# Two copies per x tile, a fourth PSUM pair for longer, and a new split of the wk copies

## The chip, the cores and the metric

The kernel runs on one core of one Trainium2 chip. The time is the device time of one execution in microseconds (us), and lower is better. A profile's span is about 1.8 us shorter than the time of its execution (288.8 us and 290.67 us for the kernel before). The effect looked for here is a few tenths of a per cent, so most of this study reads stretches of single traces, where a stall of 0.2 us is visible. The total time of one execution scatters by more than that.

## The reference

The kernel computes a gated mix of a linear attention (branch A) and an FFN (branch B) over the same input `x` of 2048 tokens by 640.

```python
# cut: helpers and the set-up of inputs (all bfloat16)
q, k, v = split(x @ wqkv)                       # 32 heads of 20
pq, pk  = q @ w_phi[h], k @ w_phi[h]
phi_q   = concat(softmax(pq), softmax(-pq))     # phi_k likewise
kv, z   = sum_s phi_k (x) v, sum_s phi_k
o       = (phi_q @ kv) / (phi_q . z + 1e-6)
a       = o @ wo
b       = (silu(x @ w_gate) * (x @ w_up)) @ w_down
g       = sigmoid((x * gate_w).sum(-1))
out     = g * a + (1 - g) * b
```

## The kernel before

Everything is issued from one list of loads and one list of operations. A tracker adds semaphore waits by what each operation reads and writes, PSUM by whole banks. The skill's rule is of the same kind: the Trainium skill, "PSUM — Partial Sum Buffer", section "PSUM bank collisions raise a hardware error", wants accesses of two engines kept apart by bank and quadrant, not by address. The rule explains why the change puts the two copies of an x tile in two banks.

The letters that matter: `H` warm matmuls on constants, `X t` transposes x tile t on TensorE, `U t.c` is part c of the v projection of tile t (two matmuls, one chunk of 128 input columns), `V` a whole v tile, `M m` premultiplies block m of wk with w_phi, `F b.k` is an FFN tile, `K` a k tile, `E` a step of the kv sum, `I` takes the fourth PSUM pair out of the ring because the kv sum needs it.

```python
LOADS = """
x0 w0 x1 w1 x2 w2 x3 w3 w4 f0 h k0 k1 t4 k2 k3 k4 t5 t6 t7 ... t15 q0 q1 q2 q3
q4 f1 f2
"""
# f0, f1, f2: columns 0 to 255, 256 to 895, 896 to 1727 of w_gate and w_up
ORDER = """
H0 H1 H2 H3 H4 H5 H6 H7 H8 H12 G X0 H9 H10 H11 U0.0 X1 H13 U0.1 U1.0 U1.1 X2 U0.2 U1.2 U2.0 U2.1
X3 U2.2 U0.3 U1.3 U2.3 U0.4 U1.4 U2.4 V3 Y F0.1 M1 i3 M0 I F0.0 M2 V4 M3 M4 K0 K1 S0 V6 V5 S1 P0
# ... cut
R2 E5 K9 S8 P7 R1 E6 K10 S9 V12 P8 E7 P9 K11 S10 P10 F0.8 R3 F1.10 E8 E9 K12 E10 S11 S12 K14 S14
# ... cut
"""
# ... cut
    def xpose(t):
        pr = next_pair()                  # least recently used pair of PSUM banks
        o = bankbf(2 * pr, 640)
        transposes([(o[:, c * P:(c + 1) * P], xs[:, t, c * P:(c + 1) * P]) for c in range(5)])
        copy("dve", xT[:, t, :, :].rearrange("p c k -> p (c k)"), o)
# ... cut
    def warm():
        pr = next_pair()
        c = nc.const_aps.tensor(1.0, [P, P], BF16)
        def fn():
            for _ in range(NWARM):        # NWARM = 2
                last = pe.matmul(bank(2 * pr, 0, P), lhsT=c, rhs=c, start=True, stop=True)
            return last
        run("pe", fn, [], [bank(2 * pr, 0, P)])
# ... cut
    def premult(which, m):
        # ... six small matmuls into both banks of a pair
        copy("dve" if which and m % 2 == 0 else "act", wqk[:, which, m, :]..., halves(pr))
# ... cut
    def kv_begin():
        ring["n"] = 3
```

The softmax here doesn't subtract the row's maximum and nothing guards it: scores larger than these inputs give would overflow.

## Time and profile before

| | kernel before |
|---|---|
| time | 290.92 us (median of 3; 290.85 to 291.63) |
| span of the profile | 288.81 us |
| TensorE (PE) busy | 285.2 us, 99% |
| PE's waits, as listed | 1.6 us, 0.8 of it at the start |

The profile's page, part 1 (busy us, share of the span, instructions) and part 4 (the chain that ended last):

```profile
PE 285.2 (99%) x1977; PEld 174.7 (60%) x1977; DVE 162.8 (56%) x241; ACT 147.5 (51%) x251; POOL 160.5 (56%) x125
...
PE 96%; DMA 2%; DVE 1%; SPq 0%; ACT 0%; issue 0%
```

TensorE is the bound. A matmul's busy time is modelled, so 99% doesn't mean that TensorE is at its peak, but a change can gain only where TensorE stands still or runs at half rate. The list of PE's waits (what waited, for what, us in total, times, longest):

```profile
PE ps L471 <- PEq L773: 0.8, 1, 0.8
PE ps L294 <- DMA wvg<-in_A_wqkv_dram: 0.4, 2, 0.2
PE ps L294 <- DVE wqk L318: 0.2, 1, 0.2
PE ps L294 <- DVE xT L318: 0.2, 1, 0.2
```

Where they lie shows in the timeline of PE (start, busy us, what, count, idle time before it):

```profile
4.76 0.61 PE L294 MATMUL ps<-wvg,xT 128*128 128x320 bf16 x2 [0.23 <-DMA wvg<-in_A_wqkv_dram]
5.21 0.44 PE L306 MATMUL ps<-ident,xs 128*128 128x128 bf16 x5
5.49 0.28 PE L471 MATMUL ps<-const-bfloat16-1.0 128*128 128x128 bf16 x2
5.60 0.44 PE L294 MATMUL ps<-wvg,xT 128*128 128x320 bf16 x2
6.24 0.72 PE L294 MATMUL ps<-wvg,xT 128*128 128x320 bf16 x4 [0.20 <-DVE xT L318]
6.80 0.44 PE L306 MATMUL ps<-ident,xs 128*128 128x128 bf16 x5
7.40 1.27 PE L294 MATMUL ps<-wvg,xT 128*128 128x320 bf16 x8 [0.17 <-DMA wvg<-in_A_wqkv_dram]
...
12.09 1.24 PE L294 MATMUL ps<-xT,wg 128*128 128x512 bf16 x5
...
19.43 0.47 PE L294 MATMUL ps<-wbd,wT 128*128 128x140 bf16 x6 [0.23 <-DVE wqk L318]
```

The bracketed idle time counts only from the modelled end of the matmul before. From start to start, beyond what a matmul takes when nothing stalls (138 ns for 320 columns), the stall before 6.24 is 0.36 us, that before 7.40 is 0.33 us and that before 19.43 is 0.39 us. The line at 12.09 is the first FFN tile, F0.1. I shall use it, the first k tile (19.75) and the tile F0.8 (52.15) as marks.

### The profile page before, as it was taken

What the parts mean: (1) busy time and instruction counts of PE and PEld (TensorE: products, weight loads), DVE (VectorE), ACT (ScalarE), POOL (GpSimd) and SP (SyncE); (2) the same over time, 40 slices, a digit from 0 to 9 for tenths busy, and PEclk for the clock granted to TensorE, in tenths of its full rate; (3) what the DMA queues carried; (4) which work ended last, traced back from release to release, by engine and by line L of the source; (5) the groups of instructions that cost most, each with busy time, mean ns of one, the idle gap of its engine ahead of it and who ended that gap; (6) DMA issues with size and microseconds to landing.
All of it is one profiled execution on the core that took longest, in us unless ns stands there. A gap on an engine that the chain in (4) does not pass through costs nothing.

```text
span 288.8 us, 4885 instructions
## 1 busy us (share of the span) xinstructions
PE 285.2 (99%) x1977; PEld 174.7 (60%) x1977; DVE 162.8 (56%) x241; ACT 147.5 (51%) x251; POOL 160.5 (56%) x125
## 2 busy tenths in 40 slices
PE   8999999999999999999999999999999999999997
PEld 6667777675644445557775546675454446656776
DVE  1256757486468987769992385980316799200000
ACT  1368768676674556574354663224675452234112
POOL 8276899879544798844733348450663649601000
DMA  6966789000010497302373102061020004410101
GB/s 214 174 119 129 108 229 353 5 2 1 0 49 0 75 330 137 70 10 41 62 141 85 20 0 51 2 134 57 2 50 0 2 1 82 92 45 0 48 23 48
DMA packets 48942, 21.61 MB, mean 75 GB/s; under 512 B 39384, under 2 KB 48792, under 8 KB 48920
## 3 DMA queue, kind: packets, MB, share of 16 engines
q1 hardware_dynamic: 48190, 20.62, 31.3%
q10 hardware_dynamic: 730, 0.68, 0.7%
q8 instruction: 16, 0.26, 0.4%
q14 instruction: 6, 0.05, 0.1%
HBM read 9.29 MB, written 2.62 MB: 41 GB/s over the span
## 4 chain that ended last, share of the span: by engine, by line
PE 96%; DMA 2%; DVE 1%; SPq 0%; ACT 0%; issue 0%
PE ps L294 96%; DMA wvg<-in_A_wqkv_dram 2%; SPq L348 0%; DVE wqk L318 0%; DVE hT L326 0%; ACT hT L312 0%; PE ps L306 0%; DVE osb L718 0%
## 5 line engine op out<-in xcount | busy, mean ns | idle before, releaser
L322 POOL TENSOR_TENSOR hT<-hT,us 128x512 bf16<-128x512 bf16 (+1 forms) x56 | 65.6, 1182 | 66.8 <-DVE hT L326 66.6
L326 DVE SCALAR_TENSOR_TENSOR hT<-hT,ps 128x512 bf16<-128x512 bf16 (+1 forms) x56 | 37.5, 683 | 73.5 <-ACT hT L312 61.2
L294 PE MATMUL ps<-xT,wg 128*128 128x512 bf16 x260 | 64.6, 379 | 0.0
L294 PE MATMUL ps<-xT,wu 128*128 128x512 bf16 x260 | 64.6, 379 | 0.0
L294 PE MATMUL ps<-wd,hT 128*128 128x320 bf16 (+2 forms) x462 | 63.9, 295 | 0.0
L312 ACT ACTIVATE hT<-ps 128x512 bf16<-128x512 f32 (+2 forms) x60 | 35.8, 596 | 46.5 <-PE ps L294 46.4
L322 POOL TENSOR_TENSOR ph<-eq,qc 128x1320 bf16<-128x1320 bf16 x16 | 42.4, 2648 | 26.1 <-DVE qc L631 24.0
L294 PEld LDWEIGHTS ps<-wd,hT 128*128 128x128 bf16 x462 | 44.5, 98 | 17.5 <-issue 0.2
L294 PE MATMUL ps<-wqk,xT 128*128 128x320 bf16 x320 | 47.7, 299 | 0.1
L294 PEld LDWEIGHTS ps<-xT,wu 128*128 128x128 bf16 x260 | 25.4, 98 | 30.7
L294 PEld LDWEIGHTS ps<-xT,wg 128*128 128x128 bf16 x260 | 25.0, 98 | 27.8 <-ACT oT L312 0.8
L312 ACT ACTIVATE osb<-ps,omg 128x640 bf16<-128x640 f32 (+2 forms) x17 | 12.9, 758 | 53.7 <-PE ps L294 53.7
L322 POOL TENSOR_TENSOR ekr<-ekr,krec 128x1280 bf16<-128x1280 bf16 x16 | 37.4, 2358 | 5.1 <-DVE krec L336 5.1
L294 PEld LDWEIGHTS ps<-wqk,xT 128*128 128x128 bf16 x320 | 30.5, 98 | 13.3 <-ACT us L312 0.5
L312 ACT ACTIVATE us<-ps 128x512 bf16<-128x512 f32 (+1 forms) x56 | 33.2, 593 | 0.3 <-POOL hT L322 0.2
L312 ACT ACTIVATE eq<-ps 128x640 bf16<-128x640 f32 x32 | 22.4, 704 | 17.3 <-POOL ph L322 10.4
L333 DVE TENSOR_REDUCE ksum<-ekr 128x64 f32<-128x1280 bf16 x16 | 23.5, 1470 | 10.4 <-ACT ekr L312 10.4
L312 ACT ACTIVATE ekr<-ps 128x640 bf16<-128x640 f32 x32 | 22.3, 704 | 8.6 <-PE ps L294 8.1
L294 PE MATMUL ps<-wvg,xT 128*128 128x320 bf16 (+1 forms) x160 | 24.6, 301 | 0.6 <-DMA wvg<-in_A_wqkv_dram 0.4
L333 DVE TENSOR_REDUCE qz<-eq 128x64 f32<-128x1280 bf16 x16 | 23.7, 1478 | 2.2 <-ACT eq L312 2.2
L294 PE MATMUL ps<-wog,oT 128*128 128x320 bf16 (+2 forms) x165 | 24.7, 294 | 0.0
L333 DVE TENSOR_REDUCE qw<-ez 128x64 f32<-128x1280 bf16 x16 | 23.6, 1477 | 0.0
(73 smaller groups left out, 188.6 us busy)
## 6 DMA issues: line engine op xcount, KB each, us to landing
out_dram<-osb SPq DMA_DIRECT2D x15, 160.0 KB, 1.9
wd<-in_B_w_down_dram SPq DMA_DIRECT2D x1, 2080.0 KB, 10.4
wg<-in_B_w_gate_dram SPq DMA_DIRECT2D x1, 1040.0 KB, 9.5
wu<-in_B_w_up_dram SPq DMA_DIRECT2D x1, 1040.0 KB, 10.5
wg<-in_B_w_gate_dram SPq DMA_DIRECT2D x1, 800.0 KB, 5.6
wu<-in_B_w_up_dram SPq DMA_DIRECT2D x1, 800.0 KB, 7.2
wog<-in_A_wo_dram SPq DMA_DIRECT2D x2, 375.0 KB, 7.1
wvg<-in_A_wqkv_dram SPq DMA_DIRECT2D x4, 160.0 KB, 4.5
```

The lines of the kernel that those rows point to most:

```text
L294: last = pe.matmul(o, lhsT=l, rhs=r, start=st, stop=sp_, skip_group_check=sk)
L312: return run("act", lambda: act.activation(o, i, func, scale=scale), rd, [o])
L322: return run(e, lambda: eo.tensor_tensor(o, a, b, op), [a, b], [o])
L326: return run("dve", lambda: dve.scalar_tensor_tensor(out=o, in0=a, scalar=s, in1=b, op0=op0, op1=op1), rd, [o])
L333: return run("dve", lambda: dve.tensor_reduce(o, i, AX.X, ALU.add), [i], [o])
```

## The change

The intent is to remove the stalls above. Each of x0, x1, x2 leaves PSUM in two copies, of one chunk and of four chunks, so that the first v part of the tile can follow after the small copy; the v parts are reordered for it, and one pair of warm matmuls goes. The fourth PSUM pair stays in the ring until just before the first kv sum. Of the five wk copies VectorE (DVE) takes blocks 0 and 3 instead of 0, 2 and 4, and ScalarE (ACT) the others.

```diff
 ORDER = """
-H0 H1 H2 H3 H4 H5 H6 H7 H8 H12 G X0 H9 H10 H11 U0.0 X1 H13 U0.1 U1.0 U1.1 X2 U0.2 U1.2 U2.0 U2.1
-X3 U2.2 U0.3 U1.3 U2.3 U0.4 U1.4 U2.4 V3 Y F0.1 M1 i3 M0 I F0.0 M2 V4 M3 M4 K0 K1 S0 V6 V5 S1 P0
+H0 H1 H2 H3 H4 H5 H6 H7 H8 H12 G X0 H9 H10 U0.0 X1 H11 U1.0 U0.1 U1.1 X2 U2.0 U0.2 U1.2 U2.1
+X3 U2.2 U0.3 U1.3 U2.3 U0.4 U1.4 U2.4 V3 Y F0.1 M1 i3 M0 F0.0 M2 V4 M3 M4 K0 K1 I S0 V6 V5 S1 P0
 # ... cut
-    ring = {"n": 4, "lru": [0, 1, 2, 3]}
+    ring = {"n": 4, "lru": [0, 1, 3, 2]}
 # ... cut
     def xpose(t):
         pr = next_pair()
-        o = bankbf(2 * pr, 640)
-        transposes([(o[:, c * P:(c + 1) * P], xs[:, t, c * P:(c + 1) * P]) for c in range(5)])
-        copy("dve", xT[:, t, :, :].rearrange("p c k -> p (c k)"), o)
+        for c0, c1 in (((0, 1), (1, 5)) if t < 3 else ((0, 5),)):
+            o = bankbf(2 * pr + (c0 > 0), 640)
+            transposes([(o[:, c * P:(c + 1) * P], xs[:, t, c * P:(c + 1) * P]) for c in range(c0, c1)])
+            copy("dve", xT[:, t, c0:c1, :].rearrange("p c k -> p (c k)"), o[:, c0 * P:c1 * P])
 # ... cut
-        copy("dve" if which and m % 2 == 0 else "act", wqk[:, which, m, :].rearrange("p (b c) -> p b c", b=2), halves(pr))
+        copy("dve" if which and m in (0, 3) else "act", wqk[:, which, m, :].rearrange("p (b c) -> p b c", b=2), halves(pr))
```

## The prediction

> **What bounds the kernel now.** TensorE: the page gives PE 285.2 of 288.8 us busy (99%), and the chain that ended last is 96% PE. The list of PE's waits holds 1.6 us: 0.8 at the start, 0.4 for wvg loads, 0.2 for an xT copy, 0.2 for a wqk copy. Behind 19.43 us the chain is practically PE alone, so only what lies before can shorten the kernel.
>
> From the PE timeline before 20 us (start to start; an unstalled v part, two matmuls, takes 0.276 us):
> - Last warm matmul 4.22, first v part 4.76: the load of w0 lands at 4.63; the x0 copy had ended at 4.42.
> - v part 5.74, next 6.24: 0.36 us stall for the x1 copy (0.49 us on DVE).
> - Last x2 transpose 7.02, next v part 7.40: 0.33 us stall for w2, which lands at 7.36.
> - The last wk block (19.43) waits 0.39 us for the DVE copy of wk block 2 (18.47 to 19.28), since only three PSUM pairs are in the ring.
>
> **What the change does.**
> 1. Split copies. For x0 this frees nothing, w0 gates it. x1's first copy (estimate from the 128x5 copy, 0.18 us, and the 128x640 one, 0.49: 0.24 us) lets U1.0 start near 5.76; x2's lets U2.0 run about 7.14 to 7.41. The gate at 7.36 stays, but U2.0 (0.276 us) has moved in front of it. The removed warm pair (0.11 us) also lies in front and is worth nothing. DVE gains about 0.18 us per tile while idle over 1 us. Worth: 0.26 us.
> 2. Fourth pair until the first kv sum. By the ring's order the last wk block then takes the pair of the FFN tile before it, whose DVE reader ended at 18.55 (18.27 shifted), and can start near 18.77; its own load landed at 18.54, so it just holds. Worth: nearly all of 0.39 us. From the third k tile on the ring is the same up to renaming of pairs.
> 3. New split of copies (DVE 0, 3; ScalarE 1, 2, 4). DVE's block 3 ends near 19.8, ScalarE's block 4 near 20.0; k tile 0 needs them at about 19.9 and 20.2. Narrow; worth 0 by itself.
>
> Everything after moves with PE; the later xT and wTq loads keep at least 0.4 us of slack. Sum: 0.65 us, 0.2%.
>
> **Prediction: 290.3 us, range 289.6 to 290.9.** Faster by over 2%: 1%; within 2%: 98%; slower by over 2%: 1%.
>
> **What would show it.** No PE wait for wqk; the wait for w2 at about 7.36 remains, with U2.0 just before it; PE 0.26 us earlier at the first FFN tile (11.8 instead of 12.09), 0.65 us earlier at the first k tile (19.1 instead of 19.75). Span about 288.15.
>
> **What would make it wrong.** The Trainium skill, "TensorE: Matmul & The Clock Gate", Part 1, says that TensorE starts at half clock and is released after a busy window of about 3.4 us that runs freely. The trace agrees: warm matmuls 107 ns apart, transposes 56 ns apart from 5.2 us. The new order has one warm pair fewer before w0 lands (0.2 us more idle); were the release delayed by a window, over 1 us would be lost. A small copy dearer than 0.24 us, or a k tile waiting for block 3 or 4, would eat 0.1 to 0.3. The three times of before spread over 0.78 us, more than the gain, so the sign may not show.

## The result, and the profile after

The changed kernel takes 290.69 us (median of 6; 290.24 to 291.01), the kernel before 290.86 us (median of 6; 290.07 to 291.63). The ratio is 0.9996, with a 95% interval from 0.9976 to 1.0015: the same. All ratios here are the mean time of one kernel's fast runs over that of the other's of the same rounds, so they are not quite the ratio of the medians quoted. Executions over 1.5% slower than the fastest of the same kernel are left out of the means.

The page of the changed kernel, parts 1 and 4:

```profile
PE 284.7 (99%) x1975; PEld 174.2 (60%) x1975; DVE 162.6 (56%) x243; ACT 148.1 (51%) x252; POOL 160.5 (56%) x125
...
PE 93%; SPq 4%; DMA 2%; issue 0%; DVE 0%
```

PE's waits in the changed kernel:

```profile
PE ps L472 <- PEq L774: 0.8, 1, 0.8
PE ps L294 <- issue: 0.6, 1, 0.6
PE ps L294 <- DMA wvg<-in_A_wqkv_dram: 0.6, 1, 0.6
```

The waits for the xT and wqk copies are gone from the list. One wait for the weights w0 is left, and there is a new one of 0.6 us that the list puts down to "issue", which means that the profile shows no releaser. The chain now leads back through the issues of SyncE's queue (SPq 4%) and a DMA instead of through PE alone. Next, PE's timeline of the changed kernel, the lines that answer to those of before:

```profile
4.67 0.43 PE L294 MATMUL ps<-wvg,xT 128*128 128x320 bf16 x2 [0.57 <-DMA wvg<-in_A_wqkv_dram]
4.94 0.44 PE L306 MATMUL ps<-ident,xs 128*128 128x128 bf16 x5
5.22 0.28 PE L472 MATMUL ps<-const-bfloat16-1.0 128*128 128x128 bf16 x2
5.48 1.00 PE L294 MATMUL ps<-wvg,xT 128*128 128x320 bf16 x6
6.32 0.44 PE L306 MATMUL ps<-ident,xs 128*128 128x128 bf16 x5
6.85 1.27 PE L294 MATMUL ps<-wvg,xT 128*128 128x320 bf16 x8
...
11.56 1.24 PE L294 MATMUL ps<-xT,wg 128*128 128x512 bf16 x5
...
15.43 1.24 PE L294 MATMUL ps<-xT,wu 128*128 128x512 bf16 x5
16.75 0.49 PE L294 MATMUL ps<-wbd,wT 128*128 128x140 bf16 x6
...
18.45 0.79 PE L294 MATMUL ps<-wbd,wT 128*128 128x140 bf16 x12
19.08 2.88 PE L294 MATMUL ps<-wqk,xT 128*128 128x320 bf16 x20
```

F0.1 starts 0.53 us earlier (11.56 for 12.09). Half of this is not the split's: x1's transposes already start 0.27 us earlier (4.94 for 5.21), because w0 landed 0.09 us earlier and the first v part ran at full rate in this execution (0.27 us to the transposes instead of 0.45 us). From x1's transposes to F0.1 it is 6.62 us instead of 6.88 us, so 0.26 us are gained there, as predicted. The stalls for the xT copies are shorter there, not gone: read from start to start, U1.0 still stalls 0.15 us (5.48) and U2.0 0.26 us (6.85), each behind its small copy; the list doesn't show them for the reason given above. The prediction had counted on such a rest. The last two wk blocks now run as one piece (18.45, x12). The first k tile starts 0.67 us earlier (19.08 for 19.75). So the change did what it was meant to do. Between 15.43 and 16.75 there is a stall of 0.24 us that wasn't there before: the load of wk block 2 landed at 16.70 in this execution, and at 15.90 in the trace of before.

The gain then disappears at one place. PE around F0.8, the first tile to read the third set of FFN columns, in the kernel before:

```profile
50.79 1.52 PE L294 MATMUL ps<-wqk,xT 128*128 128x320 bf16 x10
52.15 1.24 PE L294 MATMUL ps<-xT,wg 128*128 128x512 bf16 x5
```

and in the changed kernel:

```profile
50.12 1.52 PE L294 MATMUL ps<-wqk,xT 128*128 128x320 bf16 x10
52.22 1.24 PE L294 MATMUL ps<-xT,wg 128*128 128x512 bf16 x5 [0.58 <-issue]
```

The k tile before it starts 0.67 us earlier, F0.8 itself 0.07 us later. In the trace's semaphore events PE's sequencer waits from 50.07 to 52.17 us for the load of the last columns of w_up, which lands at 52.13. In the kernel before the same wait ended at 51.47 (landing 51.44), while PE still had work queued until 52.15. So the slack was about 0.65 us there, and the shift used it up; in addition the load came 0.69 us later. It took both: with the load as early as in the trace of before, F0.8 would have lost about 0.05 us (an estimate: TensorE could have begun it at 52.15 - 0.67 = 51.48 us, and 0.09 us, the time from landing to first matmul in after, behind a landing at 51.44 is 51.53 us). In the 12 traces of the table below the last large load lands between 51.10 and 52.50 us. The Trainium skill, "DMA: Bandwidth & Descriptors", section "Why a DMA increments its semaphore by 16 and not by 1", says that a transfer runs on up to 16 engines that finish independently, and that only the full count means that all has landed. The trace agrees: of the 16 increments of this load 14 came by 50.34, one at 50.98 and the last at 52.13. The three large loads before it in this trace show the same lag of 1.8 us between the 14th increment and the last (44.31, 46.56 and 49.44 us are their landings), so what was late was late from the first of them on.

One thing was overlooked, and no run tests it. F0.8 begins with five w_gate matmuls, whose columns had landed at 49.44 us, but `fitem` passes the w_gate and the w_up matmuls to one call of `mm`, which waits for both loads before the first of them. The w_gate matmuls take 1.08 us. Had the wait for w_up stood behind them, it would have been over before they were (an estimate: they could have run from 51.48 to 52.56 us, and the load landed at 52.13).

Behind F0.8 the two traces are alike: 234.56 us to the start of the last matmul in each, and 2.1 us from there to the end. The sum of differences is -0.53 (to F0.1) -0.14 (to the first k tile) +0.74 (to F0.8) = +0.07 us, which is the difference of the spans, 288.88 against 288.81.

### The profile page after: what moved, and what is told of

It is laid out like the page before. It is cut to its first block, busy times and chain, and to the rows that moved or that the text cites. A ratio compares the mean times of both kernels' runs of the same rounds, so it can differ in the third digit from the quotient of the medians.

```text
span 288.9 us, 4883 instructions
## 1 busy us (share of the span) xinstructions
PE 284.7 (99%) x1975; PEld 174.2 (60%) x1975; DVE 162.6 (56%) x243; ACT 148.1 (51%) x252; POOL 160.5 (56%) x125
## 4 chain that ended last, share of the span: by engine, by line
PE 93%; SPq 4%; DMA 2%; issue 0%; DVE 0%
PE ps L294 93%; SPq L347 2%; DMA wT<-in_A_wqkv_dram 2%; SPq L348 1%; DVE osb L719 0%; PE ps L306 0%
```

## The experiments

Theory L (load gate): the shift is real, and TensorE gives it back by waiting for the last FFN load. Theory C (clock): in every trace of the table below TensorE runs at half rate at first and at full rate later; I call the step the release of the clock. The changed order has lost the idle time in which a late release of TensorE's clock did no harm, so part of the gain is lost in some executions. The rival of both is that the early shift is a chance of one execution, or that the gain is lost elsewhere.

All kernels gave correct results. Each has five rounds (five or six executions with the profiled one), and the first execution of each was the profiled one. The first four ran on one chip, the next four on another and the last four on a third, each batch with its own 11 runs of the kernel before. This table splits the traces; it is read from start to start. The profiled executions of a_after_again and e_warm_more were slow ones and are left out. "Full rate from" is the first of two matmuls in a row that follow each other at full rate (56 ns for 128 columns, against 107 at half rate; the first two matmuls of all, about 60 ns apart in every trace, don't count). "x1 to F0.1" is the part of F0.1's time from the first x1 transpose on.

| kernel | x order | full rate from | w0 lands | F0.1 | x1 to F0.1 | to first k tile | to F0.8 or its stand-in | to last matmul | tail | span |
|---|---|---|---|---|---|---|---|---|---|---|
| before | old | 5.21 | 4.63 | 12.09 | 6.88 | 7.66 | 32.40 | 234.56 | 2.10 | 288.81 |
| c_before_loads | old | 5.19 | 4.63 | 12.14 | 6.95 | 7.66 | 32.40 | 234.56 | 2.09 | 288.86 |
| h_pair_only | old | 6.31 | 3.94 | 12.04 | 7.05 | 7.27 | 32.39 | 234.57 | 2.09 | 288.37 |
| after | new | 3.69 | 4.54 | 11.56 | 6.62 | 7.52 | 33.14 | 234.56 | 2.09 | 288.88 |
| b_after_loads | new | 4.59 | 3.92 | 11.18 | 6.59 | 7.27 | 32.39 | 234.56 | 2.33 | 287.75 |
| d_after_tiles | new | 4.76 | 4.31 | 11.36 | 6.61 | 7.50 | 32.39 | 234.56 | 2.09 | 287.92 |
| g_split_only | new | 4.96 | 4.04 | 11.35 | 6.69 | 7.66 | 32.41 | 234.56 | 2.09 | 288.07 |
| i_after_warm | new | 5.70 | 3.97 | 11.91 | 6.84 | 8.05 | 32.40 | 234.56 | 2.09 | 289.02 |
| b2_after_loads | new | 6.38 | 4.22 | 12.02 | 7.18 | 7.27 | 32.39 | 234.56 | 2.23 | 288.48 |
| j_best | new | 7.10 | 4.41 | 12.46 | 7.38 | 7.39 | 32.40 | 234.56 | 2.10 | 288.91 |
| k_cold | new | 8.80 | 4.29 | 12.93 | 8.02 | 7.27 | 32.39 | 234.56 | 2.10 | 289.25 |
| f_warm_less | new | 4.65 | 4.03 | 12.54 | 7.89 | 7.27 | 32.39 | 234.56 | 3.74 | 290.51 |

### First batch: is it the load?

**a_after_again.** No edit.

> The changed kernel again, for the same chip as the other three. Load theory: TensorE is about 0.6 to 0.7 us ahead of the kernel before up to 51 us, then waits for the last of the four large FFN loads (w_up, columns 896 to 1727), which lands at 51.4 to 52.2 us whatever TensorE does; the first FFN tile that reads it starts within 0.1 us of the landing; span 288.4 to 289.0. Rival (the gain was never there, the early shift is a chance of this one execution): first k tile not about 0.6 us earlier than 19.75. Ratio 0.9985 to 1.000 under either.

Measured: the profiled execution took 608.59 us. In it even two neighbouring FFN groups of five matmuls start 2.33 us apart, against 1.08 us in the kernel before (timeline of PE, a_after_again):

```profile
18.14 2.50 PE L294 MATMUL ps<-xT,wg 128*128 128x512 bf16 x5
20.47 2.50 PE L294 MATMUL ps<-xT,wu 128*128 128x512 bf16 x5
```

The slowness is there among the first warm matmuls, which are the same in both kernels (from 1.07 us on they start alternately 60 and about 163 ns apart, where before has 107 throughout), so I don't put it down to the change. This trace can't test theory L. The five fast executions took 290.18 to 293.18 us, three of them over 291.4, and one of those (293.18) had a mean granted clock of 0.994. The ratio is 1.0032 (1.0005 to 1.0059), which missed the expected 0.9985 to 1.000 and led to theory C.

**b_after_loads.** The large FFN loads change places.

```diff
-q4 f1 f2
+q4 f2 f1
```

> The changed kernel with the two pairs of large FFN loads issued in the other order (the columns that tile F0.8 reads first). Load theory: the wait at 51.3 us is gone, F0.8 starts near 51.5, span about 288.1 to 288.3, 0.6 to 0.75 us under the kernel before, ratio 0.9975. Rival (the gain is given back elsewhere, or is noise): the span stays at 288.8 and a wait of about 0.7 us stands at another place behind 52 us.

Measured in the profile: no wait before F0.8, and a span of 287.75 us, 1.06 us under before. PE around F0.8:

```profile
49.49 1.52 PE L294 MATMUL ps<-wqk,xT 128*128 128x320 bf16 x10
50.85 1.24 PE L294 MATMUL ps<-xT,wg 128*128 128x512 bf16 x5
```

and the whole list of PE's waits of this kernel:

```profile
PE ps L472 <- PEq L774: 0.8, 1, 0.8
```

So theory L holds for the trace: with the load out of the way F0.8 follows at once, and nothing is given back behind it. But the times don't follow: 290.19 us median (289.53 to 291.84), ratio 1.0001 (0.9983 to 1.0019). The expected ratio of 0.9975 lies outside the interval. The profiled execution was the fastest of its six, and one was over 291.4.

**c_before_loads.** The same edit in the kernel before.

> The kernel before with the same order of loads. Load theory: in its trace the load landed about 0.6 us before TensorE needed it, so nothing to gain: span 288.8, ratio 1.000 (down to 0.999 if the load was late in some executions). Rival (the load order is worth 0.6 us by itself, whatever the change): span about 288.2, ratio 0.998.

Measured: span 288.86 us, time 290.83 us (290.63 to 291.17), ratio 1.0011 (0.9999 to 1.0023). As expected, the order of the loads gains nothing where TensorE arrives later than the load. Stalls at the old places are in the trace, though the first has another cause: 0.55 us for w1, which landed only at 6.09 us, 0.20 us for the x2 copy, and 0.39 us before the last wk block.

**d_after_tiles.** Loads in the old order; the tiles F0.8 and F0.5 change places, so that the tile at that place reads columns that landed long ago.

```diff
-R2 E5 K9 S8 P7 R1 E6 K10 S9 V12 P8 E7 P9 K11 S10 P10 F0.8 R3 F1.10 E8 E9 ...
+R2 E5 K9 S8 P7 R1 E6 K10 S9 V12 P8 E7 P9 K11 S10 P10 F0.5 R3 F1.10 E8 E9 ...
-... A4 F1.5 F0.5 F0.10 ...
+... A4 F1.5 F0.8 F0.10 ...
```

> The changed kernel with loads in the old order, but tiles F0.8 and F0.5 changing places, so that the first FFN tile behind 51 us reads columns of the earlier pair of loads (landed by 46.6). Load theory: same as with the loads changed round: no wait at 51.3 us, span 288.1 to 288.3, ratio 0.9975. If only the load order helped and this did not, the cause would not be the wait for this load but the load order's effect on DMA or memory traffic.

Measured: no wait there, 32.39 us from the first k tile to this tile, span 287.92 us; times 290.23 us median (289.69 to 291.14), ratio 0.9993 (0.998 to 1.0005); the expected 0.9975 lies outside the interval here too. This was meant to confirm in another way that it was the wait for this load, but the trace can't: the load isn't always late, and here the last w_up load landed at 51.10, before TensorE came (51.26), so F0.8 would have waited hardly at all in its old place. (In b_after_loads the last large load landed at 51.19, and F0.8 started at 50.85, so there the exchange did take a wait away.) The gate costs its full 0.7 us only where the load lands as late as in the trace of after. In this trace another load is felt: wk block 4 landed at 18.50, and the last wk block stalled 0.23 us for it.

### Second batch: the parts, and the clock

**e_warm_more.** b_after_loads with four more warm matmuls before the first v part.

```diff
-    def warm():
+    def warm(n):
-            for _ in range(NWARM):
+            for _ in range(n):
-        "H": lambda i: warm(), ...
+        "H": lambda i: warm(6 if i == 10 else NWARM), ...
```

> The changed kernel with the loads changed round and four more warm matmuls between the x0 transposes and the first v part, so that TensorE is busy until about 4.3 us. Clock theory (some executions of the changed kernel lose 1 us and more, as the 293.18, 291.64, 291.63 and 291.84 of the last runs, because TensorE is idle longer before the first v part and its clock is released later): no execution over 291.0, median near 290.1, ratio near 0.9975. Rival (the slow executions are chance, of any kernel on any chip): again one or two of six at 291 and more, ratio near that of the kernel without the additional warm matmuls.

Measured: the profiled execution was again an odd slow one (332.94 us). The five others took 289.65 to 290.78 us; the ratio of the fast runs is 0.9981 (0.9967 to 0.9994). None is over 291.0, as theory C has it, but five executions are few, and none of the five has a trace.

**f_warm_less.** b_after_loads with five warm matmuls fewer: `warm(1 if i in (8, 9, 10, 11, 12) else NWARM)`.

> The same with five warm matmuls fewer instead (two of them before the x0 transposes). Clock theory: more executions at 291 and over, or a late release in the profile (matmuls still at half rate behind 5 us); ratio 1.000 or more. Rival: median near 290.1, ratio near 0.9975 as without the edit, since all of these matmuls lie before the load of w0 lands.

Measured: 291.65 us median (289.62 to 292.29), ratio 1.0028 (1.0005 to 1.0052), five of six over 291.4. On the same chip this interval lies wholly above that of e_warm_more, so warm matmuls that lie in front of the load gate (nine more in e_warm_more) do matter to the times. The profile, however, doesn't show the late release that theory C expected of it: full rate from 4.65 us. It is slow for two other reasons: w1 landed only at 6.72 us, and the last output transfer landed 1.6 us later than usual, at 3.74 us behind the last matmul instead of 2.1. PE's timeline of f_warm_less:

```profile
5.20 0.45 PE L294 MATMUL ps<-wvg,xT 128*128 128x320 bf16 x2
6.76 0.72 PE L294 MATMUL ps<-wvg,xT 128*128 128x320 bf16 x4 [1.11 <-DMA wvg<-in_A_wqkv_dram]
```

Why the other slow executions were slow can't be seen, since only one execution per kernel has a trace.

**g_split_only.** c_before_loads with the split copies, the new order of v parts and the new start of the ring alone (the first hunk of the order and `xpose` of the diff above; `I` and the wk copies as before).

> The kernel before with the loads changed round and part 1 alone (split copies of x0 to x2 and their order of v parts; pair ring and wk copies as before). Sum theory of the prediction: 0.26 us earlier at the first FFN tile, in any case 0.25 to 0.6, depending on when w0 and w2 land, and a stall of 0.39 us before the last wk block remains; span about 288.5, ratio 0.999.

Measured in the profile: F0.1 at 11.35 us, 0.74 us earlier than before, outside the 0.25 to 0.6 expected. Of this, 0.55 us is there before x1's first transpose (4.66 for 5.21; w0 landed at 4.04 here and at 4.63 in before), and 0.19 us behind it. The stall of 0.39 us before the last wk block is still there, and the step to the first k tile is 7.66 us as before. Span 288.07 us. In the times nothing is left of it: 290.66 us median (289.83 to 291.0), ratio 0.9998 (0.9984 to 1.0012).

**h_pair_only.** c_before_loads with the other half alone.

```diff
-... Y F0.1 M1 i3 M0 I F0.0 M2 V4 M3 M4 K0 K1 S0 ...
+... Y F0.1 M1 i3 M0 F0.0 M2 V4 M3 M4 K0 K1 I S0 ...
-        copy("dve" if which and m % 2 == 0 else "act", ...
+        copy("dve" if which and m in (0, 3) else "act", ...
```

> The kernel before with the loads changed round and parts 2 and 3 alone (fourth pair until the first kv sum, new split of wk copies; v parts as before). Sum theory: first FFN tile as before (about 12.1), no stall before the last wk block, first k tile 0.39 us nearer to it (7.27 instead of 7.66 us behind the first FFN tile), span about 288.4, ratio 0.9987.

Measured: F0.1 at 12.04 us, the first k tile 7.27 us behind it, so exactly the 0.39 us expected; span 288.37 us. Times 290.12 us median (289.82 to 290.34), ratio 0.998 (0.9967 to 0.9993). This half is shown to gain (with the loads changed round, which gained nothing by itself in c_before_loads, on another chip). The interval runs from 0.2 to 1.0 us, so it doesn't tell 0.39 from more. And one thing was unexpected: the clock was released late here, at 6.31 us, and F0.1 wasn't later for it. Part of the reason is that w0 landed 0.69 us earlier than in before, at 3.94 us. The first v part could use only 0.28 us of this, since it waited for the undivided x0 copy, which ended at 4.42 us (PE's timeline of h_pair_only):

```profile
4.48 0.71 PE L294 MATMUL ps<-wvg,xT 128*128 128x320 bf16 x2
```

### Third batch: repeats on one chip, and the extreme

**b2_after_loads.** b_after_loads again.

> The changed kernel with the loads changed round once more, now on the chip of the next three. The first profiled execution of the first kernel of a call has been an odd slow one twice (608.59 and 332.94 us); should it be odd again, it is the place in the call and not the kernel. The others: near 290.2, and by the clock theory one or two of five at 291 or more.

Measured: 290.34 us median (289.98 to 292.23), ratio 0.9995 (0.9967 to 1.0023), one of six over 291.4. The profile is the most useful, since it is the same kernel as b_after_loads in an execution with a late release. PE's timeline of b_after_loads:

```profile
4.14 0.61 PE L294 MATMUL ps<-wvg,xT 128*128 128x320 bf16 x2
4.59 0.44 PE L306 MATMUL ps<-ident,xs 128*128 128x128 bf16 x5
4.87 0.28 PE L472 MATMUL ps<-const-bfloat16-1.0 128*128 128x128 bf16 x2
5.13 1.00 PE L294 MATMUL ps<-wvg,xT 128*128 128x320 bf16 x6
5.96 0.44 PE L306 MATMUL ps<-ident,xs 128*128 128x128 bf16 x5
...
11.18 1.24 PE L294 MATMUL ps<-xT,wg 128*128 128x512 bf16 x5
```

and of b2_after_loads:

```profile
4.36 0.69 PE L294 MATMUL ps<-wvg,xT 128*128 128x320 bf16 x2
4.84 0.74 PE L306 MATMUL ps<-ident,xs 128*128 128x128 bf16 x5
5.37 0.42 PE L472 MATMUL ps<-const-bfloat16-1.0 128*128 128x128 bf16 x2
5.59 1.37 PE L294 MATMUL ps<-wvg,xT 128*128 128x320 bf16 x6
6.80 0.44 PE L306 MATMUL ps<-ident,xs 128*128 128x128 bf16 x5
...
12.02 1.24 PE L294 MATMUL ps<-xT,wg 128*128 128x512 bf16 x5
```

The first v part starts 0.22 us later. Then the transposes of x1 take 0.53 us from the first of them to the warm pair instead of 0.28, and six v matmuls take 1.21 us to the next transposes instead of 0.83, since they run at half rate. Together F0.1 is 0.84 us later, and 11.18 has become 12.02, nearly the 12.04 to 12.14 of the old order.

**i_after_warm.** e_warm_more with the loads in the old order.

> The changed kernel with the loads in the old order and the four additional warm matmuls. Load theory: a wait at 51.3 us for the last FFN load again, up to 0.75 us, median 290.3 to 290.7, so 0.2 to 0.6 us over the next kernel. If the warm matmuls alone were the lost gain: median near 290.0 as with both.

Measured: 290.09 us median (289.78 to 290.98), ratio 0.998 (0.9955 to 1.0005). Theory L had expected 290.3 to 290.7 and a wait at 51 us. The wait isn't there: TensorE came to F0.8 only at 52.36, and the load had landed at 51.81. TensorE was late because wk block 4 landed at 19.60. PE's timeline of i_after_warm at that place:

```profile
18.55 0.48 PE L294 MATMUL ps<-wbd,wT 128*128 128x140 bf16 x6
19.64 0.49 PE L294 MATMUL ps<-wbd,wT 128*128 128x140 bf16 x6 [0.61 <-DMA wT<-in_A_wqkv_dram]
```

So in the traces the load gate at F0.8 is one place of several at which a late load takes the gain, and over six executions the order of the large loads makes no difference that these runs resolve.

**j_best.** e_warm_more, and wk block 2 is loaded ahead of the x rows of tile 4.

```diff
-... f0 h k0 k1 t4 k2 k3 k4 t5 ...
+... f0 h k0 k1 k2 t4 k3 k4 t5 ...
```

> Candidate: the changed kernel, large loads changed round, four warm matmuls more, and wk block 2 loaded before the x rows of token tile 4. No wait for a load behind 10 us except up to 0.2 us before the last wk block; first k tile 7.27 us behind the first FFN tile; median 289.9 to 290.1, ratio 0.998 or below.

Measured: 290.28 us median (289.76 to 290.81), ratio 0.9986 (0.9964 to 1.0008), a little over the expected 289.9 to 290.1 us and 0.998. The trace has no stall at wk block 2 and one of 0.11 us at wk block 4. The clock was released at 7.10 us, and F0.1 came at 12.46. It isn't shown to beat h_pair_only or e_warm_more.

**k_cold.** b_after_loads with `warm(1)`, 13 warm matmuls in all.

> The changed kernel, loads changed round, every warm pair cut to one matmul (13 in all). Clock theory: the profile shows matmuls at half rate until 6 us or later, the first FFN tile about 1 us later than the 11.2 to 11.4 of the kernel with pairs, and the times lie at 291 and more. Rival (the clock's release does not depend on the warm matmuls, and the slow times of the run with five fewer had another cause): full rate from about 4.7 us, times near 290.2.

Measured: 290.98 us median (290.58 to 292.8), ratio 1.0026 (0.9996 to 1.0055), so it isn't shown to be slower than the kernel before, and three of six lie under the expected 291. The clock is released at 8.80 us, and F0.1 starts at 12.93, 1.75 us later than in b_after_loads. Here theory C is seen at work in a trace: with two steps of 0.88 and 0.61 us between matmuls before 3.3 us, both ended by loads (0.24 and 0.11 us with pairs, all from start to start), the release came 1.7 us later than in any other trace of the table, and each matmul at half rate went straight into the time of F0.1. It is one execution.

### What the experiments say together

The table's columns on F0.1 are the main finding. F0.1 itself mixes two things: when x1's transposes start, which moves with w0's landing, and the time from there on. In the new order the second, "x1 to F0.1", follows the release of the clock: 6.62, 6.59, 6.61, 6.69, 6.84, 7.18, 7.38, 8.02 us for a release at 3.69, 4.59, 4.76, 4.96, 5.70, 6.38, 7.10, 8.80. (In f_warm_less w1 set it.) In the old order it is 6.88 and 6.95 us for a release at 5.2, and 7.05 us for one at 6.31. So a release 1.1 us later costs the old order 0.17 us (before, h_pair_only), and one 1.8 us later costs the same kernel in the new order 0.59 us (b_after_loads, b2_after_loads). The old order has longer stalls for copies and loads there, and a late release partly hides in them; the new order has shortened the stalls, and with them the cover. From x1 on the gain of the split is therefore 0.19 to 0.36 us where the release comes by 5 us, and nothing at 6.4 us (7.18 against 7.05).

Before x1 the split of x0 counts too where w0 lands early: with w0 at 3.92 and 4.04 us the first v part starts at 4.14 and 4.17 us in the new order (b_after_loads, g_split_only), and at 4.48 us in the old one with w0 at 3.94 (h_pair_only). I have no trace of the old order with a release before 5.2 us or after 6.3 us, and all of this compares different executions, in which w1 and w2 landed at different times too.

Over all fast executions, those over 291.4 us were 2 of 39 of the kernel before, 0 of 10 of c_before_loads and h_pair_only, 5 of 34 of the new order with its own number of warm matmuls (after, a, b, d, g, b2), 0 of 17 with four more, and 7 of 12 with fewer. That fewer warm matmuls are slower is shown by the times of f_warm_less; that the clock is the reason isn't, since its one trace has an early release. That four more help is not shown: the two fast traces with them have a release at 5.70 and 7.10 us, later than most with the kernel's own number, and in i_after_warm the four held the first v part back to 4.54 us though w0 had landed at 3.97. Nor is it shown why the times of the new order gain so little over six executions: with the wait at F0.8 taken away they gain nothing that these runs resolve (1.0001, 0.9993 and 0.9995 in b, d and b2).

## Why the prediction was right or wrong

The time was right: 290.69 us lies in the range of 289.6 to 290.9, "within 2%" was right, and so was the warning that the sign might not show. But the range also holds the 290.86 us of the kernel before, so to hit it says nothing about the gain. The expected gain of 0.65 us didn't come in the times, and the span is 288.88 us instead of 288.15. By steps:

- **TensorE bounds the kernel, and only stalls before 19.43 us can be won.** The first half is right. The second overlooked that behind 19.43 us TensorE may start to wait where it didn't before.
- **Gain of the fourth pair, "nearly all of 0.39 us", and the copies' split worth 0.** The sum is right: 7.66 became 7.27 us in four traces of changed kernels and in h_pair_only, and no k tile waited for wk block 3 or 4. The two parts were never run apart, so that the copies' split is worth 0 is not shown. But "its own load landed at 18.54, so it just holds" holds only at times: the load of block 4 cost 0.23 us in d_after_tiles and 0.77 us (start to start) in i_after_warm, and block 2 cost 0.24 us in after, which I hadn't reckoned with.
- **Gain of the split copies, "0.26 us".** Right in after from x1's transposes on (6.62 us for 6.88). The other 0.27 us of the 0.53 us at F0.1 were luck: an earlier w0 and an early release of the clock. What was wrong is "For x0 this frees nothing, w0 gates it". I took w0's landing at 4.63 us for a fixed gate; in the fast traces it landed at 3.92 to 4.63 us, and where it is early the small x0 copy frees about 0.3 us, while with a late release the gain from x1 on is lost (7.18 us in b2_after_loads). w2's landing at 7.36 us was no fixed gate either (6.53 to 7.59 us in the other fast traces, in those of the new order before TensorE came to it). The first small copy took 0.23 us (0.24 estimated), so that part held.
- **"Everything after moves with PE; the later xT and wTq loads keep at least 0.4 us of slack."** This is the step that failed. I checked the x and wq loads and not the FFN loads. The last w_up load had only about 0.65 us of slack in the trace of before, and in after, where it landed 0.69 us later as well, it took back 0.74 us. b_after_loads, which takes that wait away, has no such loss; in d_after_tiles the load came in time.
- **The warm pair "is worth nothing".** Neither shown nor refuted for the one pair, which was never run alone. Half as many warm matmuls went with the latest release of all (k_cold, one trace), and five fewer with slower times (f_warm_less). The prediction named this risk.

What stays open: the mean gain of the split order in executions without a trace (g_split_only: 0.9998, with an interval of 0.0028), why five of six executions of f_warm_less were slow, why one of the 16 increments of each large load came more than a microsecond behind the next-to-last in after, and what the two odd slow executions were. Each of these was the profiled first execution of the first kernel of a batch; the first kernel of the third batch had none.

## What to carry to other kernels

When a change moves the bounding engine ahead, check every later load for slack against the full shift, above all the last ones of a long load queue, since they don't move with the engine. Read landing times from more than one execution before taking one for a gate. When a tile reads two loads, look whether its first matmuls wait for the second one without need. And at the start of a kernel, idle time that looks like a loss may be what a late clock release hides in: once the stalls are shortened, matmuls at half rate cost time. More warm matmuls were not shown to cure that here. Compare such changes from a mark behind the first loads, and judge by the distribution of times, not by one profile.

## What the Trainium skill lacked or had wrong

- "TensorE: Matmul & The Clock Gate", Part 1, says that the release comes about 4 us into sustained activity, give or take 500 ns from run to run. In 11 traces here with matmuls from 0.84 us on (k_cold left out) full rate began between 3.69 and 7.10 us, a spread of 3.4 us, and in two executions of the same kernel at 4.59 and 6.38 us. The first matmuls here have gaps of up to 0.8 us for loads, so it is not quite the page's case; the spread fits the page's own free-running window of 3413 ns better than its 500 ns. With 13 warm matmuls and idle gaps it began at 8.80 us.
- The same page says not to fit to a count of cold matmuls, since the penalty is under 1% of a typical kernel. It agrees in size (F0.1 between 11.18 and 12.02 us in the same kernel, 0.3% of the time), but it doesn't say that this scatter is larger than the gain of a late tuning step, and that less of it falls on the time where the start has stalls (0.17 us in the old order, 0.59 us in the new).
- "DMA: Bandwidth & Descriptors" says that the engines of a transfer finish independently, but gives no size for it. Here 14 of 16 increments of one 1040 KB load came within 0.25 us (50.09 to 50.34) and the last 1.8 us later (52.13).
- No page that I looked at gives the pattern of the two odd executions, in which TensorE was slow up to the end with a recorded clock of 1.0: 608.59 and 332.94 us here, against 290 to 293 us otherwise.
